# Two-layer MoE behind sliding-window attention on one core: twelve later attention pairs grouped two at a time in the same PSUM banks, values ahead of scores

## Chip, core and metric

The kernel runs on one core of a Trainium2 chip. Its time is the device time of one execution in microseconds (us); less is better. TensorE (PE) multiplies matrices into PSUM, which is split into banks; VectorE (DVE) and ScalarE (ACT) read PSUM and compute on SBUF; SyncE (SP) issues the DMAs.

## The reference

```
def _attn_ref(q, k, v):            # 4 batches, 8 heads, 576 positions, 64 per head
    scores = scale * q @ k^T       # heads 0 to 3: window of 32 positions; heads 4 to 7: 32 positions in steps of 4
    scores = where(mask, scores, -1e9); scores -= max(scores)
    attn = exp(scores); attn = attn / (sum(attn) + 1e-9)
    return attn @ v
def _moe_ref(x, w_in, w_out):      # 2304 tokens, 512 wide, 2048 hidden
    h = maximum(x @ w_in, 0)
    return h * h @ w_out
def _moe2_ref(x, w_in, w_out):
    h = x @ w_in
    return (h * cos(h)) @ w_out
```

The output is `_moe2_ref(_moe_ref(attention))`, all in float32.

## The kernel before, in words

**The products.** The tokens are cut into five blocks of 512, 384, 512, 512 and 384. For each layer and block the hidden dimension is walked in 16 slices `fc`. `product1` (L402) makes one slice of h from 12 matmuls, `middle` applies the activation on ACT and DVE, `product2` (L458) adds the slice into four banks of y with 12 matmuls; it is called in two halves of 6. A float32 product is three matmuls, because each operand is split into a high part (`xh`, `gh`, `w..hi`) and a remainder (`xl`, `gl`, `..lo`). The weights are split on the way in by `split_w`: a DVE chain (L153, L156, L159), a cast on ACT (L162) and a subtraction on DVE (L164). The first layer's 32 weight tiles are split while early attention and the first block run.

**Attention.** A unit is 192 positions of one pair of heads; a pair of units (`two_units(u)`, units u and u + 3) is worked on together. The six pairs of the first batch come ahead of the first block. The other 18, called later pairs here, are laid between the products of blocks one to four. Each runs in steps: scores (24 matmuls, L242, into two banks); mask and scale on DVE into the tile `p` (two instructions, L324), then a maximum (L328); exponentials on ACT (L333); normalisation (L340, L341, and L345 on ACT or L348 on DVE); three transposes (L355, one bank); a copy of them on ACT into a tile of its own, `pts` (L363); values (24 matmuls, L255, two banks); `tokens_out`, which casts the result into `xh` on ACT (L291) and writes the remainder `xl` on DVE (L294). A group of these matmuls between two big ones is called a burst below. The trace shows two records for each of the 24 matmuls, so a burst of 24 reads x48 there.

**Banks and tiles.** `bank()` hands out the four banks of pool `ps_h`, which scores, transposes, values and `product1` share. `p` and `pts` have one buffer each.

**Order.** Every step is an event with a time in units of slices: slice `fc` of block k starts at 16 k + fc. `PLACES` gives the start of each later pair; a pair's values stand 0.003 behind the scores of the pair after it, its transposes two slices after its own start (or half a slice ahead of the next pair), and the first half of `product2` at .5 of a slice, the second at .75. Between times 0 and 96 a scheduler may reorder instructions of an engine, except that the matmuls wrapped in `pe(...)` keep the program's order. Each engine then works through its list in order, and a semaphore wait holds what stands behind it.

Of the kernel before, what the change touches and what calls it, by code (L numbers as in the profile page):

```python
# [7 lines left out]
F32 = mybir.dt.float32  # L8
# [82 lines left out]
def attention_moe_moe(ctx: ExitStack, tc: tile.TileContext, units, windows, masks, w1, w2, out):  # L91
# [24 lines left out]
    def at(t, f, *a):  # L116
        events.append((t, len(events), f, a))
# [9 lines left out]
    def early(i):  # L127

        return dict(tag=f"w{NF - 1 - i // 2}_{1 - i % 2}", name="early")
# [53 lines left out]
    vals = {}  # L183
    early_units = [u for u in range(N_EARLY) if u // NG % 2 == 0]

    def load_unit(u):
        hp = u % UNITS // NG
        if u >= N_EARLY:
            t = upool.tile([P, UQ + UK], F32, tag="uq", name="uq")
# [22 lines left out]
    def bank():  # L212
        return ps_h.tile([P, 512], F32, tag="h", name="h")
# [16 lines left out]
    def mask_of(u):  # L230
        m0 = MASK_OF[u % UNITS // NG >= NPAIR // 2][u % NG] * HK
        return mask[:, m0:m0 + TPU * HK]
# [26 lines left out]
                            start=True, stop=True,  # L259
                        ))  # L260

    def pieces(u):

        b, hp, g = u // UNITS, u % UNITS // NG, u % NG
        p0 = g * TPU * QT
        done = 0
        while done < TPU * QT:
            if hp >= NPAIR // 2:
                r, i0 = divmod(p0 + done, S // DIL)
                n, step = min(TPU * QT - done, S // DIL - i0), DIL  # L270
                t0 = b * S + DIL * i0 + r
            else:
                n, step = TPU * QT - done, 1
                t0 = b * S + p0 + done
            k = max(i for i in range(NB) if STARTS[i] <= t0)
            t0 -= STARTS[k]
            n = min(n, -(-(SIZES[k] - t0) // step))
            yield k, slice(t0, t0 + (n - 1) * step + 1, step), slice(done, done + n)
            done += n

    def tokens_out(u, outs):

        c = u % UNITS // NG
        parts = []
        for n, pv in outs:
            for k, to, of in pieces(u):
                xh, xl = (t[:, c:c + n, to] for t in block(0, k))
                parts.append((xh, xl, pv[:, :, of]))
            c += n
# [6 lines left out]
    def two_units(u):  # L296

        us = u, u + NG
        first = u < N_EARLY
        at_y = early_units.index(u) if first else None  # L300
        T2 = 2 * TPU
        xs2 = [loaded.pop(i) for i in us]
        if u == 0:
            fill(7)
        banks = [bank() for _ in us]
        ss = [s[:, :TPU * HK] for s in banks]
        scores(ss, xs2, first)
        if first:
            for s in ss:
                nc.tensor.matmul(s, ident16, mask_of(u), start=False, stop=True)  # L310
            fill(FILL[0][at_y])
        yield
        nm = stat.tile([P, TPU, 2], F32, tag="nm", name="nm")
        if first:
            p = wpool.tile([P, TPU, 2, HK], F32, **early(PLACE["p", at_y % 3]))
            s = [tiles(s) for s in ss]
            for n in range(2):
                nc.vector.tensor_reduce(
                    out=nm[:, :, n], in_=s[n], axis=AX.X, op=ALU.max, negate=True)
            nc.vector.tensor_scalar(out=nm, in0=nm, scalar1=SCALE, scalar2=None, op0=ALU.mult)  # L320
        else:
            p = ppool.tile([P, TPU, 2, HK], F32, tag="p", name="p")
            for n, s in enumerate(ss):
                nc.vector.scalar_tensor_tensor(  # L324
                    out=p[:, :, n], in0=tiles(s), scalar=SCALE,
                    in1=tiles(mask_of(u)), op0=ALU.mult, op1=ALU.add)
            s = p[:, :, 0], p[:, :, 1]
            nc.vector.tensor_reduce(out=nm, in_=p, axis=AX.X, op=ALU.max, negate=True)  # L328
        yield
        sm = stat.tile([P, TPU, 2], F32, tag="sm", name="sm")  # L330
        for n in range(2):
            for i in range(TPU):
                nc.scalar.activation(  # L333
                    out=p[:, i, n], in_=s[n][:, i], func=AF.Exp,
                    scale=SCALE if first else 1.0, bias=nm[:, i, n:n + 1],
                    accum_out=sm[:, i, n:n + 1])
        yield
        rs = stat.tile([P, T2], F32, tag="rs", name="rs")
        flat = lambda t: t.rearrange("p i n -> p (i n)")
        nc.vector.tensor_scalar(out=rs, in0=flat(sm), scalar1=EPS, scalar2=None, op0=ALU.add)  # L340
        nc.vector.reciprocal(out=rs, in_=rs)  # L341
        p = p.rearrange("p i n k -> p (i n) k")
        if u in with_weights:
            for i in range(T2):
                nc.scalar.activation(  # L345
                    out=p[:, i, :], in_=p[:, i, :], func=AF.Copy, scale=rs[:, i:i + 1])
        else:
            nc.vector.tensor_tensor(  # L348
                out=p, in0=p, in1=rs.unsqueeze(2).to_broadcast([P, T2, HK]), op=ALU.mult)
        yield  # L350
        pt_bank = y_bank(0) if first else bank()
        pt = pt_bank[:, :UP]
        p = p.rearrange("p (i n) k -> p i (n k)", n=2)
        for i in range(TPU):
            pe(nc.tensor.transpose(pt[:, i * P:(i + 1) * P], p[:, i], ident))  # L355
        if first:
            fill(FILL[1])
        yield
        if first:
            pts = wpool.tile([P, UP], F32, **early(PLACE["pts", at_y % 2]))  # L360
        else:
            pts = ptpool.tile([P, UP], F32, tag="pts", name="pts")
        nc.scalar.copy(out=pts, in_=pt)  # L363
        yield
        if first:
            pv = ps_e.tile([P, 2, 512], F32, tag="e", name="e")[:, :, :UQ]
            pvs = [pv[:, n] for n in range(2)]
        else:
            pvs = [bank()[:, :UQ] for _ in us]
        values(pvs, vals.pop(u), pts.rearrange("p (i q) -> p i q", i=TPU))  # L370
        yield
        for _ in tokens_out(u, [(2, pv)] if first else [(1, pv.unsqueeze(1)) for pv in pvs]):
            if first:
                yield
        yield

    running = {}
# [145 lines left out]
    def needed(u):  # L523
        b, hp, g = u // UNITS, u % UNITS // NG, u % NG
        t = b * S + (g * TPU * QT if hp < NPAIR // 2 else 0)
        return max(i for i in range(NB) if STARTS[i] <= t)


    later = sorted(
        (u for u in range(N_EARLY, UNITS * B) if u % UNITS // NG % 2 == 0),  # L530
        key=lambda u: (needed(u), u))


    place = [t - 0.01 for t in PLACES]
    with_weights = {u for u, t in zip(later, place) if t < NF}

    def later_by(t, d):

# [9 lines left out]
        return t  # L548
    for u, times in zip(early_units, EARLY_TIMES):
        in_steps([before(t) for t in times], u, two_units, u)  # L550
    for i, u in enumerate(later):
        t, t2 = place[i:i + 2]
        tr = min(t + TRANS, t2 - 0.5)
        in_steps([t, *(later_by(t, d) for d in (0.15, 0.75, 0.8)), tr, later_by(tr, 0.1),
                  t2 + 0.003, later_by(t2, 0.42)], u, two_units, u)
        for n in range(2):
            at(later_by(t, -1.5 + 0.1 * n) if i else before(49), load_unit, u + n * NG)
        at(later_by(t, 0.6) if i else before(49), load_values, u)


    def some(table, i, times):
# [131 lines left out]
```

## Time and profile before

| what | value |
|---|---|
| median of 3 runs | 864.4 us (864.31 to 864.66) |
| profiled execution | 865.89 us; its span 864.1 us |
| PE busy | 852.7 us, 99% of the span |
| DVE busy | 505.5 us, 58% |
| ACT busy | 434.7 us, 50% |
| granted TensorE clock, mean | 0.996 of full speed |

The span runs from the first to the last instruction; the other 1.8 us lie around it. A busy PE here means that matmuls follow each other without a gap in the records; it does not say that each is useful. The 18 later pairs lie between 45 and 327 us of the span; behind that stand only products.

### The profile page before, as it was taken

What the parts mean: (1) busy time and instruction counts of PE and PEld (TensorE: products, weight loads), DVE (VectorE), ACT (ScalarE), POOL (GpSimd) and SP (SyncE); (2) the same over time, 40 slices, a digit from 0 to 9 for tenths busy, and PEclk for the clock granted to TensorE, in tenths of its full rate; (3) what the DMA queues carried; (4) which work ended last, traced back from release to release, by engine and by line L of the source; (5) the groups of instructions that cost most, each with busy time, mean ns of one, the idle gap of its engine ahead of it and who ended that gap; (6) DMA issues with size and microseconds to landing.
All of it is one profiled execution on the core that took longest, in us unless ns stands there. A gap on an engine that the chain in (4) does not pass through costs nothing.

```text
span 864.1 us, 15506 instructions
## 1 busy us (share of the span) xinstructions
PE 852.7 (99%) x6242; PEld 743.7 (86%) x6248; DVE 505.5 (58%) x980; ACT 434.7 (50%) x1061; POOL 47.9 (6%) x84
## 2 busy tenths in 40 slices
PE   7999999999999999999999999999999999999998
PEld 4778889999888888889999888899988888888998
DVE  5899954454443353225999974556555555555554
ACT  6667764443433332224555654555554545455554
POOL 0000000000000000000000110111111111111110
PEclk9899999999999999999999999999999999999999
DMA  7767612221311120003564400020020002000101
GB/s 285 260 218 268 229 59 90 75 78 39 102 52 39 36 98 1 1 1 132 193 229 153 152 19 1 22 77 1 1 86 1 0 1 86 1 0 1 50 1 37
DMA packets 24711, 68.59 MB, mean 79 GB/s; under 512 B 2624, under 2 KB 8512, under 8 KB 24640
## 3 DMA queue, kind: packets, MB, share of 16 engines
q1 hardware_dynamic: 24352, 67.38, 23.3%
q8 instruction: 49, 0.80, 0.4%
q10 hardware_dynamic: 288, 0.23, 0.1%
q14 instruction: 22, 0.18, 0.1%
HBM read 58.16 MB, written 9.44 MB: 78 GB/s over the span
## 4 chain that ended last, share of the span: by engine, by line
PE 95%; DVE 2%; ACT 1%; DMA 1%; issue 0%; SPq 0%
PE y L458 45%; PE h L402 44%; PE h L255 2%; PE h L242 2%; DMA early<-units 1%; PE h L355 1%; PE e L255 1%; DVE wt L159 1%; DVE wt L156 0%; DVE w L164 0%; ACT early L333 0%; PE y L355 0%; DVE wt L153 0%; DVE xl L294 0%; DVE gl L444 0%
## 5 line engine op out<-in xcount | busy, mean ns | idle before, releaser
L458 PE MATMUL y<-gh,w 128*128 128x512 f32 (+1 forms) x1280 | 401.6, 371 | 0.0
L402 PE MATMUL h<-xh,w 128*128 128x512 f32 (+1 forms) x1280 | 394.2, 369 | 0.0
L402 PEld LDWEIGHTS h<-xh,w 128*128 128x128 f32 x1280 | 238.2, 188 | 31.1 <-DVE p L324 0.4
L458 PEld LDWEIGHTS y<-gh,w 128*128 128x128 f32 x1280 | 237.6, 188 | 30.3
L402 PE MATMUL h<-xl,w 128*128 128x512 f32 (+1 forms) x640 | 235.8, 368 | 0.3 <-DVE xl L294 0.3
L458 PE MATMUL y<-gl,w 128*128 128x512 f32 (+1 forms) x640 | 235.3, 368 | 0.0
L444 DVE TENSOR_TENSOR gl<-r,gh 128x512 fp32r<-128x512 f32 (+1 forms) x160 | 102.5, 641 | 132.8 <-ACT gh L442 132.7
L433 DVE TENSOR_TENSOR r<-h,r 128x512 f32<-128x512 f32 (+1 forms) x128 | 81.9, 641 | 165.1 <-ACT r L430 94.6
L402 PEld LDWEIGHTS h<-xl,w 128*128 128x128 f32 x640 | 120.4, 188 | 16.0 <-DVE xl L294 0.7
L458 PEld LDWEIGHTS y<-gl,w 128*128 128x128 f32 x640 | 120.2, 188 | 14.3 <-DVE gl L444 0.2
L442 ACT CAST gh<-r 128x512 fp32r<-128x512 f32 (+1 forms) x160 | 92.3, 577 | 75.1 <-PE y L458 64.4
L429 ACT ACTIVATE r<-r 128x512 f32<-128x512 f32 (+1 forms) x80 | 47.1, 590 | 145.4 <-DVE r L426 145.4
L414 ACT ACTIVATE r<-h 128x512 f32<-128x512 f32 (+1 forms) x80 | 44.3, 554 | 96.8 <-PE h L402 96.6
L421 POOL TENSOR_SCALAR kf<-kf 128x512 f32<-128x512 f32 (+1 forms) x80 | 47.7, 596 | 805.3 <-ACT kf L420 801.8
L420 ACT ACTIVATE kf<-h,magic 128x512 f32<-128x512 f32 (+1 forms) x80 | 51.1, 639 | 21.8 <-PE h L402 21.6
L430 ACT ACTIVATE r<-r,halfpi 128x512 f32<-128x512 f32 (+1 forms) x80 | 54.3, 681 | 2.4
L424 DVE SCALAR_TENSOR_TENSOR r<-kf,h 128x512 f32<-128x512 f32 (+1 forms) x80 | 49.9, 625 | 4.7 <-POOL kf L421 4.7
L426 DVE SCALAR_TENSOR_TENSOR r<-kf,r 128x512 f32<-128x512 f32 (+1 forms) x80 | 50.9, 638 | 2.5
L162 ACT CAST w<-wt 128x512 fp32r<-128x512 f32 x64 | 39.4, 619 | 24.5 <-DVE wt L159 24.4
L164 DVE TENSOR_TENSOR w<-wt,w 128x512 fp32r<-128x512 f32 x64 | 43.4, 684 | 5.2 <-ACT w L162 5.1
L159 DVE SCALAR_TENSOR_TENSOR wt<-wraw,wt 128x512 uint32<-128x512 uint32 x58 | 40.4, 699 | 0.3
L156 DVE SCALAR_TENSOR_TENSOR wt<-wraw,wt 128x512 uint32<-128x512 uint32 x58 | 39.9, 689 | 0.8
(55 smaller groups left out, 395.3 us busy)
## 6 DMA issues: line engine op xcount, KB each, us to landing
wraw<-w SPq DMA_DIRECT2D x58, 512.0 KB, 4.0
uq<-units SPq DMA_DIRECT2D x36, 208.0 KB, 3.6
uv<-windows SPq DMA_DIRECT2D x18, 384.0 KB, 4.6
early<-w SPq DMA_DIRECT2D x6, 512.0 KB, 4.4
y<-o SPq DMA_DIRECT2D x6, 512.0 KB, 2.8
xraw<-y SPq DMA_DIRECT2D x6, 512.0 KB, 5.0
out<-o SPq DMA_DIRECT2D x6, 512.0 KB, 2.8
early<-units SPq DMA_DIRECT2D x6, 416.0 KB, 6.1
```

The source lines that it names most:

```text
L159: nc.vector.scalar_tensor_tensor(out=t, in0=low, scalar=29, in1=t, op0=ALU.logical_shift_right, op1=ALU.bitwise_or)
L402: pe(nc.tensor.matmul(h, w[:, c * P:(c + 1) * P], x[:, c, :], start=c == 0 and i == 0, stop=c == NC - 1 and i == 2))
L420: nc.scalar.activation(out=kf, in_=h, func=AF.Identity, bias=magic, scale=INV2PI)
L421: nc.gpsimd.tensor_scalar(out=kf, in0=kf, scalar1=-MAGIC, scalar2=1.0, op0=ALU.add, op1=ALU.mult)
L424: nc.vector.scalar_tensor_tensor(out=r, in0=kf, scalar=-C1, in1=h, op0=ALU.mult, op1=ALU.add)
L426: nc.vector.scalar_tensor_tensor(out=r, in0=kf, scalar=-C2, in1=r, op0=ALU.mult, op1=ALU.add)
L429: nc.scalar.activation(out=r, in_=r, func=AF.Abs)
L430: nc.scalar.activation(out=r, in_=r, func=AF.Sin, bias=halfpi, scale=-1.0)
L433: nc.vector.tensor_tensor(out=r, in0=h, in1=r, op=ALU.mult)
L442: nc.scalar.copy(out=gh, in_=r)
L444: nc.vector.tensor_tensor(out=gl, in0=r, in1=f32(gh), op=ALU.subtract)
L458: pe(nc.tensor.matmul(y[e], w[:, e * P:(e + 1) * P], g, start=fc == 0 and n == 0, stop=fc == NF - 1 and n == 2,))
```

## The change

Twelve of the later pairs form six groups of two; six stay single: 12, 13, 18, 19, 20 and 38. A function `group(us)` takes the place of `two_units` for later pairs. A group's two units share two banks for scores and two for values; their transposes take a bank each. The tile `pts` is gone: transposes are copied back into `p`, which holds one or two pairs and still has one buffer. Values are called 0.003 ahead of the next group's scores. `PLACES` has 13 entries in place of 19, and the first six are the old ones. The transposes' time is now the start plus one slice and one for each pair. For a single pair whose successor starts two slices later, that time lies just behind the values' time; as the steps of a pair are resumed in order, the step resumed ahead of the next scores is then the transposes, and values follow 0.1 of a slice later. Normalisation of the fifth and sixth later pairs goes to DVE. Every later pair's exponentials, copies and stores remain, in other batches.

```diff
-PLACES = (3.75, 6.75, 8.75, 10.75, 12.75, 14.75, 17.75, 20.75, 22.75, 25.75, 27.75, 30.75, 33.75, 36.75, 39.75, 42.75, 45.75, 48.75, 51.75)
-TRANS = 2
+GROUPS = ((12,), (13,), (18,), (19,), (20,), (14, 24), (30, 31), (32, 25), (26, 36), (42, 43), (44, 37), (38,))
+PLACES = (3.75, 6.75, 8.75, 10.75, 12.75, 14.75, 20.75, 25.75, 30.75, 36.75, 42.75, 46.75, 51.75)
...
-    ptpool = pool("pt", 1)
...
+    def group(us):
+
+        parts = [slice(a * TPU, (a + 1) * TPU) for a in range(len(us))]
+        ss = [bank()[:, :len(us) * TPU * HK] for _ in range(2)]
+        for u, i in zip(us, parts):
+            scores([s[:, i.start * HK:i.stop * HK] for s in ss],
+                   [loaded.pop(n) for n in (u, u + NG)], False)
+        yield
+        p = ppool.tile([P, len(us) * TPU, 2, HK], F32, tag="p", name="p")
+        nm = stat.tile([P, len(us) * TPU, 2], F32, tag="nm", name="nm")
+        for n, s in enumerate(ss):
+            for u, i in zip(us, parts):
+                nc.vector.scalar_tensor_tensor(
+                    out=p[:, i, n], in0=tiles(s)[:, i], scalar=SCALE,
+                    in1=tiles(mask_of(u)), op0=ALU.mult, op1=ALU.add)
+        nc.vector.tensor_reduce(out=nm, in_=p, axis=AX.X, op=ALU.max, negate=True)
+        yield
+        sm = stat.tile([P, len(us) * TPU, 2], F32, tag="sm", name="sm")
+        for i in parts:
+            exponentials(p[:, i], (p[:, i, 0], p[:, i, 1]), nm[:, i], sm[:, i], 1.0)
+            yield
+            normalize(rows_of(p[:, i]), flat(sm[:, i]), us in with_weights)
+            yield
+        pts = [bank()[:, :UP] for _ in us]
+        for pt, i in zip(pts, parts):
+            transposes(pt, p[:, i])
+        yield
+        for pt, i in zip(pts, parts):
+            nc.scalar.copy(out=p[:, i].rearrange("p i n k -> p (i n k)"), in_=pt)
+        yield
+        pvs = [bank()[:, :len(us) * UQ] for _ in range(2)]
+        for a, (u, i) in enumerate(zip(us, parts)):
+            values([pv[:, a * UQ:(a + 1) * UQ] for pv in pvs], vals.pop(u),
+                   p[:, i].rearrange("p i n k -> p i (n k)"))
+        yield
+        for _ in tokens_out(us, [(1, pv.unsqueeze(1)) for pv in pvs]):
+            pass
         yield
...
-    with_weights = {u for u, t in zip(later, place) if t < NF}
+    with_weights = {us for us, t in zip(GROUPS, place) if t < NF - 4}
...
-    for i, u in enumerate(later):
+    for i, us in enumerate(GROUPS):
         t, t2 = place[i:i + 2]
-        tr = min(t + TRANS, t2 - 0.5)
-        in_steps([t, *(later_by(t, d) for d in (0.15, 0.75, 0.8)), tr, later_by(tr, 0.1),
-                  t2 + 0.003, later_by(t2, 0.42)], u, two_units, u)
...
+        by = lambda d: later_by(t, d)
+        soft = [by(0.15)] + [by(d + a) for a in range(len(us)) for d in (0.75, 0.8)]
+        tr = t + 1 + len(us)
+        in_steps([t, *soft, tr, later_by(tr, 0.1), t2 - 0.003, later_by(t2, 0.42)],
+                 us, group, us)
```

In the order of the engines' lists the change reads as follows; names are those of the kernel. PE first, where the third later pair's scores come in (in the kernel before, at 78 us of the trace): the rows before.

```order
L458 MATMUL y_795<-gh,w_1_1025 128x512
L458 MATMUL y_795<-gl,w_1_1025 128x512
L458 MATMUL y_795<-gh,w_1_1025 128x512
L242 MATMUL h<-uq 32x64 x24
L255 MATMUL h<-pts,uv 64x32 x24
L458 MATMUL y_796<-gh,w_1_1025 128x512
L458 MATMUL y_796<-gl,w_1_1025 128x512
L458 MATMUL y_796<-gh,w_1_1025 128x512
L458 MATMUL y_797<-gh,w_1_1025 128x512
L458 MATMUL y_797<-gl,w_1_1025 128x512
L458 MATMUL y_797<-gh,w_1_1025 128x512
L402 MATMUL h<-xh_364,w_0_1048 128x512
```

And the same place after the change: the second half of `product2` (L497 in the changed file) ends a slice, and `product1` (L441) begins the next.

```order
L335 MATMUL h<-ident,p 128x128 x3
L241 MATMUL h<-uq 32x64 x24
L497 MATMUL y_793<-gh,w_1_1021 128x512
L497 MATMUL y_793<-gl,w_1_1021 128x512
L497 MATMUL y_793<-gh,w_1_1021 128x512
L497 MATMUL y_794<-gh,w_1_1021 128x512
L497 MATMUL y_794<-gl,w_1_1021 128x512
L497 MATMUL y_794<-gh,w_1_1021 128x512
L254 MATMUL h<-p,uv 64x32 x24
L441 MATMUL h<-xh_361,w_0_1044 128x512
L441 MATMUL h<-xl_362,w_0_1044 128x512
```

The transposes moved from ahead of the first half of that `product2` to the burst, and the values from the burst to the end of the slice, directly ahead of `product1`. This holds at four places: behind the scores of the third, fourth and fifth later pair and of the first group of two. With the waits shown, the end of that piece reads so (`DVE_49` is the semaphore that DVE raises, `Activation_49` that of ACT):

```order
L497 MATMUL y_794<-gh,w_1_1021 128x512
L254 MATMUL h<-p,uv 64x32 [waits DMAHW3_49,Activation_49]
L254 MATMUL h<-p,uv 64x32
L254 MATMUL h<-p,uv 64x32 [waits PE_49]
L254 MATMUL h<-p,uv 64x32 x21
L441 MATMUL h<-xh_361,w_0_1044 128x512 [waits DVE_49]
L441 MATMUL h<-xl_362,w_0_1044 128x512
```

In the kernel before, `product1` at this place also waits for DVE, but half a `product2` stands between it and the burst. The instruction that raises DVE's semaphore here is the first of the two that read the new scores' banks into `p`. On DVE, before the change, they stand so (L324, with waits; the L156, L159 and L153 rows around them split weights):

```order
L156 SCALAR_TENSOR_TENSOR wt<-wraw,wt 128x512 [waits DVE_49]
L153 TENSOR_SCALAR wt<-wraw 128x512 [waits DMAHW6_49,DVE_49]
L159 SCALAR_TENSOR_TENSOR wt<-wraw,wt 128x512 [waits DVE_49]
L324 SCALAR_TENSOR_TENSOR p<-h,given 128x3x64 [waits PE_49] x2
L156 SCALAR_TENSOR_TENSOR wt<-wraw,wt 128x512 [waits DVE_49]
L328 TENSOR_REDUCE nm<-p 128x6 [waits DVE_49]
```

After the change (L389 are the same two instructions; L152, L155, L158 and L163 split weights):

```order
L155 SCALAR_TENSOR_TENSOR wt<-wraw,wt 128x512 [waits DVE_49]
L152 TENSOR_SCALAR wt<-wraw 128x512 [waits DMAHW6_49,DVE_49]
L158 SCALAR_TENSOR_TENSOR wt<-wraw,wt 128x512 [waits DVE_49]
L155 SCALAR_TENSOR_TENSOR wt<-wraw,wt 128x512 [waits DVE_49]
L158 SCALAR_TENSOR_TENSOR wt<-wraw,wt 128x512 [waits DVE_49]
L163 TENSOR_TENSOR w_0_1227<-wt,w_0_1227 128x512 [waits Activation_49]
L389 SCALAR_TENSOR_TENSOR p<-h,given 128x3x64 [waits PE_49]
L389 SCALAR_TENSOR_TENSOR p<-h,given 128x3x64
L483 TENSOR_TENSOR gl<-r,gh 128x512 [waits Activation_49]
```

Three more weight-splitting instructions stand ahead of the two, and the two wait for the last of PE's values, as they write `p`, from which the values are read. At the next such place, the fourth later pair's, the remainder `gl` of the slice (L483) stands directly ahead of them, and it waits for ACT's cast `gh`:

```order
L155 SCALAR_TENSOR_TENSOR wt<-wraw,wt 128x512 [waits DVE_49]
L163 TENSOR_TENSOR w_1_1510<-wt,w_1_1510 128x512 [waits Activation_49]
L483 TENSOR_TENSOR gl<-r,gh 128x512 [waits Activation_49]
L389 SCALAR_TENSOR_TENSOR p<-h,given 128x3x64 [waits PE_49]
L389 SCALAR_TENSOR_TENSOR p<-h,given 128x3x64
```

At the fifth pair's place the row ahead of the two is the same `gl`; at that of the first group of two it is the same `gl` once more, and there are four such instructions instead of two, two for each bank.

Counted over PE's list, the bursts of the later pairs change as follows. Before there are 37: 18 of transposes alone, 17 of scores and values, one of scores alone and one of values alone. After there are 25: one of scores (the first pair), two of transposes (the first pair's and the last pair's), six of a group's transposes, four of transposes and scores, four of values alone (the four places above), one of a single pair's values with the next scores, five of a group's values with the next group's scores, one of a group's values with the last pair's scores, and one of values (the last pair's). In blocks two to four nothing but these bursts differs on PE.

## Rows read from the trace of the kernel before

**Rows 1.** The page, busy time of each engine (share of the span) and instructions.

```profile
PE 852.7 (99%) x6242; PEld 743.7 (86%) x6248; DVE 505.5 (58%) x980; ACT 434.7 (50%) x1061; POOL 47.9 (6%) x84
```

**Rows 2.** Windows: length, busy PE, PEld, DVE, ACT, POOL, granted clock, DMA share, GB/s.

```profile
65.00:87.00 22.00, 22.00 (x276) 17.87 (x260) 21.93 (x51) 16.83 (x55) 0.00 (x0) 1.00 0.78 263
...
109.00:131.00 22.00, 22.00 (x193) 18.43 (x192) 10.79 (x26) 14.50 (x53) 0.00 (x0) 1.00 0.14 43
```

**Rows 3.** Timeline of PE: start, length, operation; from one big matmul to another.

```profile
70.56 0.39 PE L402 MATMUL h<-xh,w 128*128 128x512 f32 x1
...
73.28 0.39 PE L458 MATMUL y<-gh,w 128*128 128x512 f32 x1
73.51 0.39 PE L402 MATMUL h<-xh,w 128*128 128x512 f32 x1
...
148.76 0.33 PE L458 MATMUL y<-gl,w 128*128 128x384 f32 x1
148.93 0.34 PE L458 MATMUL y<-gh,w 128*128 128x384 f32 x1
```

**Rows 4.** Timeline of PE: scores alone, between two big matmuls and behind.

```profile
45.43 0.39 PE L458 MATMUL y<-gh,w 128*128 128x512 f32 x1
45.75 0.75 PE L242 MATMUL h<-uq 64*32 64x64 f32 x48
46.44 0.50 PE L458 MATMUL y<-gh,w 128*128 128x512 f32 x1
46.77 0.40 PE L458 MATMUL y<-gl,w 128*128 128x512 f32 x1
```

**Rows 5.** Timeline of PE: scores and values in one burst, and what follows.

```profile
64.78 0.76 PE L242 MATMUL h<-uq 64*32 64x64 f32 x48
65.46 0.90 PE L255 MATMUL h<-pts,uv 64*64 64x32 f32 x48
66.30 0.50 PE L458 MATMUL y<-gh,w 128*128 128x512 f32 x1
...
67.56 0.40 PE L458 MATMUL y<-gh,w 128*128 128x512 f32 x1
67.93 0.50 PE L402 MATMUL h<-xh,w 128*128 128x512 f32 x1
```

**Rows 6.** Timeline of PE: transposes alone, ahead of the third later scores.

```profile
76.00 0.39 PE L402 MATMUL h<-xh,w 128*128 128x512 f32 x1
76.23 0.49 PE L355 MATMUL h<-ident,p 128*128 128x128 f32 x3
76.47 0.48 PE L458 MATMUL y<-gh,w 128*128 128x512 f32 x1
76.79 0.39 PE L458 MATMUL y<-gl,w 128*128 128x512 f32 x1
```

**Rows 7.** Timeline of DVE: masking instructions (L324); releaser in brackets.

```profile
67.53 0.35 DVE L324 SCALAR_TENSOR_TENSOR p<-h,given 128x192 f32<-128x192 f32 x1
...
79.42 0.68 DVE L159 SCALAR_TENSOR_TENSOR wt<-wraw,wt 128x512 uint32<-128x512 uint32 x1
80.02 0.61 DVE L324 SCALAR_TENSOR_TENSOR p<-h,given 128x192 f32<-128x192 f32 x2
80.55 0.68 DVE L156 SCALAR_TENSOR_TENSOR wt<-wraw,wt 128x512 uint32<-128x512 uint32 x1
...
117.78 0.62 DVE L324 SCALAR_TENSOR_TENSOR p<-h,given 128x192 f32<-128x192 f32 x2 [1.81 <-PE h L242]
```

**Rows 8.** Timeline of PE: the scores that the last masking row waits for.

```profile
117.02 0.76 PE L242 MATMUL h<-uq 64*32 64x64 f32 x48
```

**Rows 9.** Timeline of ACT and DVE: the chain from `gh` to `gl`.

```profile
73.76 0.62 ACT L442 CAST gh<-r 128x512 fp32r<-128x512 f32 x1 [0.42 <-PE y L458]
...
108.30 0.61 ACT L442 CAST gh<-r 128x512 fp32r<-128x512 f32 x1
...
108.94 0.69 DVE L444 TENSOR_TENSOR gl<-r,gh 128x512 fp32r<-128x512 f32 x1 [0.18 <-ACT gh L442]
109.55 0.69 DVE L156 SCALAR_TENSOR_TENSOR wt<-wraw,wt 128x512 uint32<-128x512 uint32 x1
```

**Rows 10.** Timeline of ACT and DVE: storing one pair's values.

```profile
92.66 0.86 ACT L291 CAST xh<-h 128x80 fp32r<-128x80 f32 x6 [0.93 <-PE h L255]
...
94.72 1.00 DVE L294 TENSOR_TENSOR xl<-h,xh 128x80 fp32r<-128x80 f32 x5
```

More of the change, by code (lines that the diff above doesn't have):

```diff
@@ L294, in tokens_out, with normalize, exponentials @@
             nc.vector.tensor_tensor(out=xl, in0=piece, in1=f32(xh), op=ALU.subtract)
[L296 to L320, printed above, removed]
-        else:
[L322 to L330, printed above, removed]
+    def normalize(p, sm, by_scalar):
+        n = p.shape[1]
+        rs = stat.tile([P, n], F32, tag="rs", name="rs")
+        nc.vector.tensor_scalar(out=rs, in0=sm, scalar1=EPS, scalar2=None, op0=ALU.add)
+        nc.vector.reciprocal(out=rs, in_=rs)
+        if by_scalar:
+            for i in range(n):
+                nc.scalar.activation(
+                    out=p[:, i, :], in_=p[:, i, :], func=AF.Copy, scale=rs[:, i:i + 1])
+        else:
+            nc.vector.tensor_tensor(
+                out=p, in0=p, in1=rs.unsqueeze(2).to_broadcast([P, n, HK]), op=ALU.mult)
+    def exponentials(p, s, nm, sm, scale):
         for n in range(2):
@@ L334, in two_units @@
                     out=p[:, i, n], in_=s[n][:, i], func=AF.Exp,
[L335 to L353, printed above, removed]
+                    scale=scale, bias=nm[:, i, n:n + 1], accum_out=sm[:, i, n:n + 1])
@@ L354, in two_units, with transposes @@
+    flat = lambda t: t.rearrange("p i n -> p (i n)")
+    rows_of = lambda p: p.rearrange("p i n k -> p (i n) k")
+    def transposes(pt, p):
+        p = p.rearrange("p i n k -> p i (n k)")
         for i in range(TPU):
             pe(nc.tensor.transpose(pt[:, i * P:(i + 1) * P], p[:, i], ident))
-        if first:
-            fill(FILL[1])
-        yield
[L359 to L362, printed above, removed]
+    def two_units(u):
+        us = u, u + NG
+        at_y = early_units.index(u)
+        xs2 = [loaded.pop(i) for i in us]
+        if u == 0:
+            fill(7)
+        ss = [bank()[:, :TPU * HK] for _ in us]
+        scores(ss, xs2, True)
+        for s in ss:
+            nc.tensor.matmul(s, ident16, mask_of(u), start=False, stop=True)
+        fill(FILL[0][at_y])
+        yield
+        nm = stat.tile([P, TPU, 2], F32, tag="nm", name="nm")
+        p = wpool.tile([P, TPU, 2, HK], F32, **early(PLACE["p", at_y % 3]))
+        s = [tiles(s) for s in ss]
+        for n in range(2):
+            nc.vector.tensor_reduce(
+                out=nm[:, :, n], in_=s[n], axis=AX.X, op=ALU.max, negate=True)
+        nc.vector.tensor_scalar(out=nm, in0=nm, scalar1=SCALE, scalar2=None, op0=ALU.mult)
+        yield
+        sm = stat.tile([P, TPU, 2], F32, tag="sm", name="sm")
+        exponentials(p, s, nm, sm, SCALE)
+        yield
+        normalize(rows_of(p), flat(sm), False)
+        yield
+        pt = y_bank(0)[:, :UP]
+        transposes(pt, p)
+        fill(FILL[1])
+        yield
+        pts = wpool.tile([P, UP], F32, **early(PLACE["pts", at_y % 2]))
@@ L363, in two_units @@
         nc.scalar.copy(out=pts, in_=pt)
         yield
[L365 to L370, printed above, removed]
-        yield
-        for _ in tokens_out(u, [(2, pv)] if first else [(1, pv.unsqueeze(1)) for pv in pvs]):
-            if first:
-                yield
+        pv = ps_e.tile([P, 2, 512], F32, tag="e", name="e")[:, :, :UQ]
@@ L550, in attention_moe_moe @@
         in_steps([before(t) for t in times], u, two_units, u)
-    for i, u in enumerate(later):
+    for i, us in enumerate(GROUPS):
         t, t2 = place[i:i + 2]
-        tr = min(t + TRANS, t2 - 0.5)
-        in_steps([t, *(later_by(t, d) for d in (0.15, 0.75, 0.8)), tr, later_by(tr, 0.1),
-                  t2 + 0.003, later_by(t2, 0.42)], u, two_units, u)
-        for n in range(2):
-            at(later_by(t, -1.5 + 0.1 * n) if i else before(49), load_unit, u + n * NG)
-        at(later_by(t, 0.6) if i else before(49), load_values, u)
+        by = lambda d: later_by(t, d)
[3 more added lines that the diff above has]
+                 us, group, us)
+        for a, u in enumerate(us):
+            for n in range(2):
+                at(by(-1.5 + 0.1 * (2 * a + n)) if i else before(49), load_unit,
+                   u + n * NG, "uv" if a and n else "uq")
+            at(by(0.6 + 0.1 * a) if i else before(49), load_values, u)
     def some(table, i, times):
```

72 lines of the change are left out of this document (42 added, 30 removed).

## Prediction

> **What bounds the kernel now.** I read the page's busy times first: PE is busy 852.7 of 864.1 us, no other engine over 60% [rows 1]. So the change can gain only what it takes from PE's own list, and lose wherever PE is made to wait. I then read PE's timeline around attention. Big matmuls follow each other every 0.227 us in blocks of 512 (70.56 to 73.28 is 2.72 us for 12) and every 0.17 us in blocks of 384 [rows 3]. Between them a burst of scores starts 0.32 us after the big matmul before it, 0.09 more than that pace, takes 0.69 us, and the first big matmul behind it takes 0.33, 0.10 more [rows 4]. In a burst of both, values take 0.84 and follow the scores with no gap of their own [rows 5]. Transposes start at the big matmul's own pace, take 0.24 us, and cost 0.09 at the exit (0.32 for the next one) [rows 6]. So a burst costs a switch, and fewer bursts cost fewer switches. Last I read windows: between 65 and 87 us, where the third later pair stands, DVE is busy 21.93 of 22.00 us with weights; after 109 us it is half idle [rows 2]. A new wait of PE for DVE in the first stretch therefore has no slack behind it. The clock is 1.00 of full speed in both, so it moves nothing here.
>
> **The change, part by part.** *Removed switches.* Bursts of transposes alone fall from 18 to 8: ten exits of 0.09, 0.90 us. Bursts with scores or values fall from 19 to 17: two entries and exits of 0.09 + 0.10, 0.38 us. Together 1.28 us. The trace has no burst that passes from transposes to scores or from values to scores, so the price of that seam is bounded: free, as from scores to values, or an entry of 0.09 each. Eleven seams hold here (four of the first kind, seven of the second); at 0.09 each 0.99 less, so the gain lies between 0.3 and 1.3 us. I take 1.28, since the seam that the trace does show is free. The matmuls themselves stay: as many of each kind as before, and double bursts run longer at the same price. Copies and stores come in other batches on ACT and DVE, which are not the bound.
>
> *Added waits.* At four places the order is now transposes, scores, six matmuls of `product2`, values, `product1`. `product1` takes a bank of the new scores, which the first masking instruction on DVE must have read; and that instruction writes `p`, from which the values ahead of it are being read. Before, transposed values had a tile of their own, so masking ran while `product2` did. Now PE cannot begin `product1` until the values are done and masking has then run: values, masking, `product1` in series. All of PE stands behind that `product1`.
>
> The floor of that wait: masking starts when the last of the values ends, and the end of a modelled burst lies 0.07 us behind the start of the next big matmul (scores at 117.02 + 0.76 = 117.78, where masking starts [rows 7, 8]; the same burst in rows 4 gives 0.69 to the next matmul). From the start of masking to the start of `product1` it is 0.40 us: 67.53 to 67.93, where PE waited for just that at the second pair (0.37 us from the matmul before in place of 0.23) [rows 5, 7]. So no less than 0.47 us each. For the group of two there are two masking instructions on that first bank, and the first takes 0.27 (two in 0.53, 80.02 to 80.55 [rows 7]), so 0.74. Floor of all four: 3 x 0.47 + 0.74 = 2.15 us.
>
> What stands ahead of masking on DVE makes it longer. *Third pair:* before, masking began at 80.02, directly behind a weight instruction that began at 79.42, 0.60 earlier; DVE was full. Three more such instructions now stand ahead: 80.02 + 3 x 0.60 = 81.82, and `product1` at 82.22. Without the wait it would stand at 76.23 + 1.36 (six matmuls) + 0.24 + 0.09 + 0.69 + 0.10 + 1.36 + 0.09 + 0.84 = 81.00. Wait: 1.22 us. *Fourth and fifth pair:* `gl` stands ahead of masking and waits for the cast `gh`, which waits for the end of the six `product2` matmuls. Call the start of what follows these six h. The cast began 0.25 behind it (73.51 to 73.76) and runs 0.61; `gl` follows 0.03 later (108.30 + 0.61 to 108.94) and the next DVE instruction 0.61 after that (109.55) [rows 3, 9]. Masking at h + 0.25 + 0.62 + 0.03 + 0.61 = h + 1.51, `product1` at h + 1.91, where values alone would let it start at h + 0.09 + 0.84 = h + 0.93. Wait: 0.98 us each. *First group:* the same with 0.27 more, 1.25 us. Sum: 1.22 + 0.98 + 0.98 + 1.25 = 4.43 us. If DVE has one weight instruction more ahead at each place, that is 4 x 0.60 = 2.4 us more; the floor is 2.15. While PE waits, DVE and ACT work on, so the wait is not paid twice: `gl` and the activation of the next slice come no later to PE than PE itself does.
>
> A repeated gap of this sort has a line in the notes: the Trainium skill, Perfetto Trace Analysis, Identifying Performance Opportunities, says that the same gap repeating on the engine that should be saturated can mean too little SBUF or PSUM for the next tile. The trace before has no such gap on PE around the later pairs, and by that rule the one buffer of `p` would make one.
>
> *Later blocks.* Behind the first group values stand directly ahead of scores, and masking of the new scores has half a `product2` to run beside, as before. I cost those bursts at nothing; what that rests on is the third rival.
>
> **Sum.** 4.43 - 1.28 = 3.15 us on the profiled execution: 865.89 + 3.15 = 869.0. The median of the runs shown, 864.4, lies 1.5 below that execution, so 867.6 as the median after. I call 0.2% (1.73 us, 862.7 to 866.1) what a measurement here can tell from no change.
>
> **Rivals.** *Four waits of about 1 us each:* the forecast, 867.6. For it speaks that the wait is in the program, whatever the timing, and that its links are rows.
>
> *Short waits, the other side.* Place: masking behind values at the same four places. If DVE has cleared its list by then, so that only the series values, masking, `product1` is left, the waits are 2.15 us and the switches give back 1.28: +0.87, 865.3, no measurable change. Below 3.0 us of waits in all (0.75 each) the time lies within 0.2%; below 1.28 us (0.32 each) the kernel would be no slower at all, and that is under the floor. For it speaks that DVE has less to do behind 109 us; against it that `gl` there hangs on PE's own matmuls through ACT, not on DVE's load, and that at the third pair DVE has 0.07 us free in 22. Faster by over 0.2% would need no waits and more than 1.73 us from the switches, which the sum does not give; that would take some wait of before that I have not seen.
>
> *Late banks in the later blocks.* A group's values for two pairs lie in two banks, and `product1` half a slice later takes the first of them. It must have been read by casts (six in 0.86 us) and subtractions (five in 1.00, so six in 1.2) [rows 10]: about 2.1 us. PE covers that with scores of two pairs, 2 x 0.69, an exit of 0.10 and six matmuls of 0.17, 2.5 us, less 0.07 for the end of the values. That leaves 0.35 us. If one other instruction of 0.6 us stands ahead on ACT or DVE, PE waits 0.25; if two do, 0.85; over five such bursts 1.3 to 4.3 us, which makes 868.9 to 871.9. Against it: only blocks of 384 are so tight; six matmuls of 0.227 leave 0.34 more, and DVE is half idle there. A page speaks for this rival: the Trainium skill, Perfetto Trace Analysis, Matmuls (under Optimizing Tensor Performance), wants independent groups of matmuls to rotate through banks, so that reading one overlaps the next group's matmuls. Two pairs in one bank rotate less, and no row here shows what that costs.
>
> **How the numbers follow.** Four waits of about 1 us: 0.62, at 866.3 to 869.3. Short waits: 0.22, 864.9 to 866.1. Late banks on top of the four waits: 0.10. Something that makes it faster: 0.06. The range reaches from the floor's case, less 0.4 us for a larger gain at the switches, 864.9, to the forecast with one more instruction of 0.6 us at each place, 867.6 + 2.4 = 870.0, which takes in the smaller part of the late banks. Slower by over 0.2% is the first and third case, 0.72; within 0.2% the second, 0.22; faster the last, 0.06.
>
> **What would show it.** In the profile after, PE's timeline has four gaps ahead of `product1` between 78 and 135 us, each released by DVE's masking instruction, about 1.2, 1.0, 1.0 and 1.2 us, with values directly ahead of the gap and masking beginning at or after the end of the values. Transposes directly ahead of scores and values directly ahead of scores show no more than 0.1 us between them; 25 bursts cost some 1.3 us less than 37. No PE idle with a releaser stands behind 140 us; if there is, on a bank that ACT's casts or DVE's subtractions let go, it is the third rival. The prediction is wrong if masking begins within 0.1 us of the values' end at all four places (short waits), or if PE's gaps there are missing altogether, which would mean that the bank came from somewhere else than I read.

## The result and the profile after

The changed kernel takes 872.5 us (871.16 to 873.35, 6 runs) beside 864.6 us of the kernel before (6 runs): ratio 1.0086, interval 1.0074 to 1.0098. It is slower, as forecast, but by 7.9 us, more than twice the 3.2 that was forecast. The profiled execution, at 872.67 us, has a span of 870.9 us, 6.8 more than before. Busy times, by engine:

```profile
PE 851.6 (98%) x6242; PEld 743.5 (85%) x6248; DVE 503.4 (58%) x970; ACT 432.7 (50%) x1043; POOL 48.0 (6%) x84
```

PE is busy 1.1 us less than in [rows 1] and has as many instructions. So the loss is idle time of PE. The list of who PE waited for (engine, line, releaser: total us, times, longest) begins so:

```profile
PE h L441 <- DVE p L389: 5.0, 5, 1.3
PE h L241 <- issue: 2.9, 2, 1.7
PE e L254 <- issue: 1.6, 2, 1.5
```

The first line is `product1` waiting for masking. The second is new and was not forecast: scores that stop for 2.9 us in two places, released by nothing that the profile shows. (The third lies in the first 25 us, ahead of all that the change touches, where PE waits in several ways that differ from one execution to the next; its longest, 1.47 us at 22.19, comes up again below.)

**The masking gaps** stand where they were forecast. PE at the first of the four places, in order of time:

```profile
78.21 0.39 PE L497 MATMUL y<-gh,w 128*128 128x512 f32 x1
78.44 0.49 PE L335 MATMUL h<-ident,p 128*128 128x128 f32 x3
78.86 0.76 PE L241 MATMUL h<-uq 64*32 64x64 f32 x48
79.55 0.50 PE L497 MATMUL y<-gh,w 128*128 128x512 f32 x1
...
81.13 0.90 PE L254 MATMUL h<-p,uv 64*64 64x32 f32 x48
83.19 0.50 PE L441 MATMUL h<-xh,w 128*128 128x512 f32 x1 [1.16 <-DVE p L389]
```

Values take 0.84 us, so `product1` would have begun at 81.97 and is 1.22 late. DVE at the first, second and fourth place:

```profile
82.18 0.68 DVE L163 TENSOR_TENSOR w<-wt,w 128x512 fp32r<-128x512 f32 x1
82.78 0.61 DVE L389 SCALAR_TENSOR_TENSOR p<-h,given 128x192 f32<-128x192 f32 x2
...
96.62 0.69 DVE L483 TENSOR_TENSOR gl<-r,gh 128x512 fp32r<-128x512 f32 x1
97.22 0.62 DVE L389 SCALAR_TENSOR_TENSOR p<-h,given 128x192 f32<-128x192 f32 x2
...
125.64 0.69 DVE L483 TENSOR_TENSOR gl<-r,gh 128x512 fp32r<-128x512 f32 x1 [6.50 <-ACT gh L481]
126.25 1.14 DVE L389 SCALAR_TENSOR_TENSOR p<-h,given 128x192 f32<-128x192 f32 x4
```

Masking runs directly behind a weight instruction or behind `gl`, and `product1` starts 0.41 us after masking (82.78 to 83.19; 0.40 in [rows 5, 7]). At the fourth place DVE had been idle 6.5 us for `gh`.

**The new stalls** lie in bursts of two groups, 96 records of values and 96 of scores. The first such burst and the second:

```profile
154.23 0.34 PE L497 MATMUL y<-gh,w 128*128 128x384 f32 x1
154.50 1.60 PE L254 MATMUL h<-p,uv 64*64 64x32 f32 x96
156.03 1.03 PE L241 MATMUL h<-uq 64*32 64x64 f32 x75
158.24 0.43 PE L241 MATMUL h<-uq 64*32 64x64 f32 x21 [1.17 <-issue]
158.60 0.44 PE L497 MATMUL y<-gh,w 128*128 128x384 f32 x1
...
180.03 0.34 PE L497 MATMUL y<-gh,w 128*128 128x384 f32 x1
180.30 1.60 PE L254 MATMUL h<-p,uv 64*64 64x32 f32 x96
181.83 1.27 PE L241 MATMUL h<-uq 64*32 64x64 f32 x96
183.03 0.44 PE L497 MATMUL y<-gh,w 128*128 128x384 f32 x1
```

The first takes 4.37 us from one big matmul to the next, the second 3.00: 1.37 lost, after 75 of 96 records of scores. The third, at 204.78, stops after 74 for 1.68 us and loses 1.88 (4.88 in all); the fourth and fifth don't stop. No wait on a semaphore stands at these places in PE's list: the 38th of 48 matmuls is like those around it.

What is under way there is PE's own program. The page's part on DMA queues (packets, MB, share) has a row for instructions:

```profile
q8 instruction: 49, 0.80, 0.4%
```

The DMA view of 155.8 to 156.9 us, within that burst, has one of these transfers:

```profile
q8 instruction: 1, 0.02, 5.3%
```

It is one packet, on one of the 16 engines, so it took 5.3% of 16 x 1.1 us, 0.93 us; by the trace's packets it began at 155.88 and landed at 156.81. The page has 49 transfers of 16 KB. PE has 12,490 records of matmuls and weight loads, 255 for each transfer. The Trainium skill, Runtime: NRT & Kernel Launch, Instruction fetch mechanics, says that instructions come in blocks of 16 KiB, 256 each, the next fetched while the current one runs, mostly hidden. By these rows the size agrees, and hidden is what has to be tested. Counted in program order (a small float32 matmul of attention is four instructions, two weight loads and two matmuls; a big one two; a wait of its own one), the two stalls begin at PE's instructions 3,778 and 5,058: 1,280 apart, 5 x 256. (The trace has 3,772 and 5,052 records of PE ahead of them; six matmuls have left no record.) So block ends are known for every burst. A burst of two groups has 386 instructions; the first block end in it is its 87th, 215th, 85th, 163rd and 244th in the five bursts. Only in the first and third does a second one fall into the same burst, 256 later, and only these stall.

The kernel before had a small sign of it, in early attention. PE there, and at the same place after the change:

```profile
21.91 0.24 PE L255 MATMUL e<-early 64*64 64x32 f32 x2 [0.17 <-issue]
```

```profile
22.19 0.24 PE L254 MATMUL e<-early 64*64 64x32 f32 x2 [1.47 <-issue]
```

955 records of PE stand ahead of either, which is within one of 3,772 less 11 x 256, so a block end fits there too.

### The profile page after: what moved, and what is told of

Same layout as the page of the kernel before. It is cut to its first block, busy times and chain, and to the rows that moved or that the text cites. A ratio compares the mean times of both kernels' runs of the same rounds, so it can differ in the third digit from the quotient of the medians.

```text
span 870.9 us, 15484 instructions
## 1 busy us (share of the span) xinstructions
PE 851.6 (98%) x6242; PEld 743.5 (85%) x6248; DVE 503.4 (58%) x970; ACT 432.7 (50%) x1043; POOL 48.0 (6%) x84
## 4 chain that ended last, share of the span: by engine, by line
PE 88%; DVE 7%; DMA 2%; issue 2%; ACT 1%; SPq 0%; ACTq 0%; DVEq 0%
PE y L497 42%; PE h L441 42%; DVE wt L158 2%; DVE wt L155 2%; DVE w L163 1%; PE h L254 1%; PE h L241 1%; DMA early<-units 1%; DVE wt L152 1%; DVE gl L483 1%; DMA early<-windows 1%; PE h L335 1%; DMA wraw<-w 0%; PE e L254 0%; DVE xl L306 0%
## 5 line engine op out<-in xcount | busy, mean ns | idle before, releaser
L441 PE MATMUL h<-xh,w 128*128 128x512 f32 (+1 forms) x1280 | 394.6, 369 | 5.0 <-DVE p L389 5.0
L497 PE MATMUL y<-gh,w 128*128 128x512 f32 (+1 forms) x1280 | 397.9, 369 | 0.0
L441 PEld LDWEIGHTS h<-xh,w 128*128 128x128 f32 x1280 | 238.1, 188 | 36.5 <-DVE p L389 4.5
L497 PEld LDWEIGHTS y<-gh,w 128*128 128x128 f32 x1280 | 237.5, 188 | 30.5
L441 PE MATMUL h<-xl,w 128*128 128x512 f32 (+1 forms) x640 | 235.8, 368 | 0.3 <-DVE xl L306 0.3
L497 PE MATMUL y<-gl,w 128*128 128x512 f32 (+1 forms) x640 | 235.4, 368 | 0.0
L483 DVE TENSOR_TENSOR gl<-r,gh 128x512 fp32r<-128x512 f32 (+1 forms) x160 | 102.5, 641 | 128.0 <-ACT gh L481 126.6
L441 PEld LDWEIGHTS h<-xl,w 128*128 128x128 f32 x640 | 120.4, 188 | 15.8 <-DVE xl L306 0.7
L497 PEld LDWEIGHTS y<-gl,w 128*128 128x128 f32 x640 | 120.2, 188 | 15.1 <-DVE gl L483 0.6
L163 DVE TENSOR_TENSOR w<-wt,w 128x512 fp32r<-128x512 f32 x64 | 43.3, 685 | 4.8 <-ACT w L161 4.5
L325 ACT ACTIVATE p<-p,nm 128x64 f32<-128x64 f32 x108 | 36.2, 337 | 9.5 <-DVE nm L392 9.5
L158 DVE SCALAR_TENSOR_TENSOR wt<-wraw,wt 128x512 uint32<-128x512 uint32 x58 | 40.4, 700 | 0.4
```

What stands on the lines that cost most here:

```text
L158: nc.vector.scalar_tensor_tensor(out=t, in0=low, scalar=29, in1=t, op0=ALU.logical_shift_right, op1=ALU.bitwise_or)
L163: nc.vector.tensor_tensor(out=lo, in0=f32(t), in1=f32(hi), op=ALU.subtract)
L441: pe(nc.tensor.matmul(h, w[:, c * P:(c + 1) * P], x[:, c, :], start=c == 0 and i == 0, stop=c == NC - 1 and i == 2))
L483: nc.vector.tensor_tensor(out=gl, in0=r, in1=f32(gh), op=ALU.subtract)
L497: pe(nc.tensor.matmul(y[e], w[:, e * P:(e + 1) * P], g, start=fc == 0 and n == 0, stop=fc == NF - 1 and n == 2,))
```

## Experiments

Theory A, after the traces: the one buffer `p` puts values, masking and `product1` in series (gaps), and bursts of 386 small instructions outrun the fetch of PE's program (stalls). Rivals: B, DVE is full, whatever `p` does; C, the stalls come from the loads of units and windows that start in these bursts; D, values ahead of scores make masking late by themselves. Seven kernels, each timed beside the kernel before; ratios are to that one's runs on the same chip (its medians there are 866.1 and 866.3 us).

**Transposes in a tile of their own again**, for single pairs:

```diff
+    ptpool = pool("pt", 1)
...
+        q = ptpool.tile([P, TPU, 2, HK], F32, tag="pts", name="pts") if len(us) == 1 else p
         for pt, i in zip(pts, parts):
-            nc.scalar.copy(out=p[:, i].rearrange("p i n k -> p (i n k)"), in_=pt)
+            nc.scalar.copy(out=q[:, i].rearrange("p i n k -> p (i n k)"), in_=pt)
...
-                   p[:, i].rearrange("p i n k -> p i (n k)"))
+                   q[:, i].rearrange("p i n k -> p i (n k)"))
```

> The changed kernel, but the transposes of a single pair are copied into a tile of their own again, as in the kernel before; groups of two still copy into p. Theory A (one buffer p, read by the values, holds masking back, and product1 behind it): masking then stands right behind the scores in DVE's list and no longer waits for the values, so the four gaps of 1.16, 1.18, 1.08 and 1.28 us ahead of product1 fall to under 0.2 us each, and the time falls by 4 to 4.7 us, to about 868. The two stalls without a releaser at 158 and 209 us stay, some 4.5 us earlier. Rival B (the gaps come from a full DVE and from where values stand, not from p): the gaps stay at 0.7 us or more, and the time falls by less than 2 us.

867.1 us, ratio 1.0004 (0.9993 to 1.0015): no loss is left that can be told from noise. PE's waits for masking are gone entirely, and two stalls of 1.74 and 1.24 us remain at 152.97 and 203.34. PE and DVE at the first and second place:

```profile
80.24 0.90 PE L255 MATMUL h<-pts,uv 64*64 64x32 f32 x48
81.08 0.50 PE L443 MATMUL h<-xh,w 128*128 128x512 f32 x1
```

```profile
79.96 0.61 DVE L390 SCALAR_TENSOR_TENSOR p<-h,given 128x192 f32<-128x192 f32 x2
...
92.49 0.60 DVE L390 SCALAR_TENSOR_TENSOR p<-h,given 128x192 f32<-128x192 f32 x2
...
94.68 0.68 DVE L485 TENSOR_TENSOR gl<-r,gh 128x512 fp32r<-128x512 f32 x1
```

Values still stand directly ahead of `product1`, and no gap follows. DVE is as full as before (busy 21.93 us of 22.00 from 65 to 87, as in [rows 2]), but masking now runs ahead of the values, and the scheduler put it ahead of `gl` too. B falls.

**Transposes half a slice ahead of the next pair**, so that values and scores share a burst:

```diff
-        tr = t + 1 + len(us)
+        tr = min(t + 1 + len(us), t2 - 0.5)
```

> The changed kernel, but a single pair's transposes stand no later than half a slice ahead of the next pair, as before, so that its values share the burst of the next scores, values first, with half a product2 behind them; p is still copied into in place. Theory A: the four gaps of 1.1 to 1.3 us ahead of product1 fall to what the second pair shows in the changed kernel, 0.3 us each, since scores now end a burst and masking has 1.36 us of matmuls beside it; the switches of four bursts fewer give 0.1 to 0.2 us each, less four exits of transposes of 0.09. Sum: 4.7 - 1.3 = 3.4 us, and some 0.3 us: about 869. The stalls without a releaser in the first and third burst of two groups stay. Rival B (masking is late whatever stands around it because DVE is full): the gaps stay above 0.8 us, 871 or more.

867.0 us, ratio 1.0006 (0.9995 to 1.0017). The gaps fell to nothing, not to 0.3 us; the stalls were 1.23 and 1.13 us. Here `p` is still written in place: with half a `product2` behind the scores, masking has its time. The two kernels take the same loss away from either end of the series.

**Values ahead of scores in the kernel before**, nothing else:

```diff
-                  t2 + 0.003, later_by(t2, 0.42)], u, two_units, u)
+                  t2 - 0.003, later_by(t2, 0.42)], u, two_units, u)
```

> The kernel before with one edit: values stand ahead of the next scores in all of its bursts; pairs stay single and the tile of their own for transposes stays. Theory A (the order inside a burst costs nothing where half a product2 follows it): the time is within 0.2% of the kernel before, and product1 behind the bursts beside the first block starts without a gap of over 0.2 us. Rival D (scores that end later make masking late for product1, as the 0.32 us at the second pair of the changed kernel suggests): 0.3 us at each of the five bursts beside the first block, 1.5 us more.

867.2 us, ratio 1.0010 (0.9998 to 1.0021). The time alone leaves room for D's 1.5 us, but PE has no gap of over 0.2 us behind any of these bursts: D falls. The 0.32 us at the second pair of the changed kernel doesn't belong to the order: with the same instructions up to there, the kernel of the next experiment shows no gap that the list of waits names.

**Values of a group half a `product2` ahead of the next scores:**

```diff
-        in_steps([t, *soft, tr, later_by(tr, 0.1), t2 - 0.003, later_by(t2, 0.42)],
+        in_steps([t, *soft, tr, later_by(tr, 0.1), t2 - (0.25 if len(us) > 1 else 0.003), later_by(t2, 0.42)],
```

> The changed kernel, but a group's values stand half a product2 (6 matmuls) ahead of the next scores, not in their burst. Theory A (PE's instructions come in blocks of 256, fetched by DMA; a burst of 386 that crosses two block boundaries uses up a block in 1.9 us while the next takes 3.0 to 3.6 us to come): 6 matmuls between the halves give 1.04 us (384) to 1.36 us (512) and an entry and exit of 0.19, so the stalls of 1.17 and 1.68 us without a releaser shrink to 0 to 0.5 us; six more switches cost 6 x 0.19 = 1.1 us. Sum: 3.25 - 1.1 - 0.3 = 1.9 us less, 870.6 (870.0 to 871.4). Rival C (the loads of units and windows that start in those bursts hold PE up): the stalls stay at over 1 us, as the loads start at the same places, and the time rises by 1.1 us to 873.6.

870.5 us, ratio 1.0049 (1.0031 to 1.0067), span 868.6, 2.3 us under the changed kernel's. No scores wait for "issue" any more; the masking gaps stay:

```profile
PE h L441 <- DVE p L389: 4.7, 4, 1.3
PE h L241 <- DMA early<-units: 2.5, 3, 1.7
```

(The second line lies in the first 25 us.) The first burst's scores take 1.48 us in place of 1.27, so about 0.2 of its stall is left. Rival C would have kept the stalls.

**Block ends moved by 104 instructions**, put at the very start of PE's list:

```diff
-            fill(7)
+            fill(2)
+            for _ in range(57):
+                nc.tensor.matmul(spare[:, :16], idle[:, :P], idle[:, :16], start=True, stop=True)
```

> The changed kernel with 104 more small instructions on PE at the very start (5 of the 7 warm-up matmuls of 512 columns are replaced by 57 of 16 columns); nothing else moves. Theory A (block boundaries at every 256th instruction): a group's burst of 386 instructions stalls if its first boundary lies within its first 130. In the changed kernel the first boundary lies at 87, 215, 85, 163 and 244 in the five bursts of two groups, and the first and third stall. With 104 more it lies at 239, 111, 237, 59 and 140: the second and fourth stall, by 1.2 to 1.8 us (near 181 and 242 us), and the first and third no longer do. The time stays within 1 us of the changed kernel's. Rival C (loads, or what those two bursts wait for in data): the first and third burst still stall, and the second and fourth don't.

873.3 us, ratio 1.0086 (1.0062 to 1.0110). The stalls moved as forecast, from the first and third burst to the second and fourth:

```profile
180.79 0.34 PE L241 MATMUL h<-uq 64*32 64x64 f32 x9 [1.31 <-issue]
240.41 0.60 PE L241 MATMUL h<-uq 64*32 64x64 f32 x35 [1.71 <-issue]
280.54 0.39 PE L499 MATMUL y<-gh,w 128*128 128x512 f32 x1 [0.30 <-issue]
```

The second block end lies at 111 + 256 = 367 of 386 in the second burst, which leaves 19 instructions or 9.5 records (9 were left), and at 59 + 256 = 315 in the fourth, which leaves 71, 35.5 records (35). In the fifth it lies at 140 + 256 = 396, ten behind the burst, and there a big matmul waits 0.30 us. The trace has 4,540 and 5,820 records of PE ahead of the first two of these stalls; like 3,772 and 5,052, each is 188 more than a multiple of 256. The loads start in all five bursts of both kernels, whether they stall or not. C falls as the cause of the stalls. The fetch was not hidden at these places.

**Masking ahead of `gl`**, by a later time for `gl` in slices 7 to 14 of the first block and by pinning both in DVE's list:

```diff
-                steady = ([0] * (NC - 1), MIDDLE[m], (LAG[m] + 0.5, LAG[m] + 0.75))
+                mid = MIDDLE[m] if (m, k) != (0, 0) or fc not in range(7, 15) else (0.53, 0.72, 0.86, 1.93)
+                steady = ([0] * (NC - 1), mid, (LAG[m] + 0.5, LAG[m] + 0.75))
```

> The changed kernel, but DVE's list is held so that masking at the four places stands ahead of the remainder gl (two weight instructions still stand there); p is still read by the values and written by masking. Theory A (values, masking, product1 in series is the floor, and gl ahead of masking is the rest): the gaps at the second to fourth place fall from 1.18, 1.08 and 1.28 us to the floor, 0.5 to 0.8 us each, but not to 0; the first, where weight instructions stand ahead, falls by 0.3 us at most. Sum 1.3 to 1.9 us less than the changed kernel. If gl alone were the cause, the gaps at these three would go to under 0.2 us; if p alone, they would stay at 1.0 or more.

870.9 us, ratio 1.0060 (1.0041 to 1.0078). The gaps were 1.36, 0.56, 1.02 and 0.93 us, 3.9 in all in place of 4.7 at the four places; 1.3 to 1.9 less was expected. (The profiled execution took 874.5, with two stretches at a lower clock that the last section shows.) The fourth shows the series bare: DVE idle for 8.38 us, then masking on the heels of the values, and still

```profile
126.26 1.15 DVE L390 SCALAR_TENSOR_TENSOR p<-h,given 128x192 f32<-128x192 f32 x4 [8.38 <-PE h L254]
```

```profile
125.19 0.90 PE L254 MATMUL h<-p,uv 64*64 64x32 f32 x48
127.02 0.47 PE L442 MATMUL h<-xh,w 128*128 128x512 f32 x1 [0.93 <-DVE p L390]
```

a gap of 0.93 (0.99 from start of values plus 0.84), where the forecast put the floor at 0.74. At the third, weight instructions took the room of `gl`. So the floor exists; what stood on it was whatever DVE had next, and reordering DVE alone took only 0.8 us of these gaps. (By the ratios this kernel lies some 2.2 us below the changed one, with intervals that touch; the gaps account for 0.8 of it.)

**The better kernel**: transposes early as above, and values half a `product2` ahead of the scores only in the two bursts with two block ends:

```diff
-        tr = t + 1 + len(us)
-        in_steps([t, *soft, tr, later_by(tr, 0.1), t2 - 0.003, later_by(t2, 0.42)],
+        tr = min(t + 1 + len(us), t2 - 0.5)
+        in_steps([t, *soft, tr, later_by(tr, 0.1), t2 - (0.25 if i in (5, 7) else 0.003), later_by(t2, 0.42)],
```

> The changed kernel with two edits: a single pair's transposes stand half a slice ahead of the next pair, as before (this took away the four gaps behind masking), and values stand half a product2 ahead of the next scores, but only in the two bursts that cross two block boundaries of PE's instructions (those with the first and the third group of two). Theory A: no gap behind masking and no stall without a releaser; against that kernel without the split, 1.23 + 1.13 = 2.4 us of stalls go and two switches of 0.19 come: 2.0 us less, 865.0 beside 866.1 of the kernel before, so 1 to 2 us below it. Rival C (the stalls belong to what those bursts load or wait for): stalls of over 0.5 us remain, and the time stays at 867.

864.2 us beside 866.3 of the kernel before, ratio 0.9979 (0.9970 to 0.9987): faster than both kernels. One stall of 0.53 us is left in the first of the two split bursts; in the other the scores take 1.58 us in place of 1.27, so 0.3 is left there.

## Why the prediction was right and wrong

*Right:* slower, and by the mechanism named. `product1` came 1.22, 1.24, 1.14 and 1.34 us late at the four places (start of values plus 0.84, against its start), 4.9 in all, where the sum had 1.22, 0.98, 0.98, 1.25, 4.43. At the second and third place `gl` waited for DVE, not for ACT: the cast at the second began at 95.72 and was done at 96.34, `gl` began at 96.62, when DVE's weight instructions let it. So it is partly luck that 0.98 came near 1.24 and 1.14 there. The late banks of the third rival did not come: the list has no wait of PE behind the first block that names ACT's casts or DVE's subtractions. Nor did the short waits.

*Mis-sized:* the switches. I had 1.28 us; taking every burst as the time from the last big matmul ahead of it to the second one behind it, beyond their pace, and the gaps and stalls out, bursts of the later pairs cost 37.2 us before and 34.9 after, 2.3 less. The seam from transposes to scores is not free: 78.44 to 78.86 is 0.42, where transposes alone take 0.24, so it costs exit and entry in full. Six transposes in two banks cost as much as two times three. The seam from values to scores is free (65.28 to 66.11 at the second pair, 0.83). And "double bursts run longer at the same price" was wrong to the good: 96 records of values take 1.53 us, not 1.68, and 96 of scores 1.20 (181.83 to 183.03), not 1.38. I did not find why.

*The step that failed* is "I cost those bursts at nothing" for the later blocks, whose only rival was late banks. The sign named for those blocks was idle time with a releaser; what came has none. In its place, bursts of 386 instructions outrun the fetch of PE's program: the first block end is crossed near 155.2 us (87 of the 192 instructions of values, at 1.53 us for all), the transfer shows between 155.8 and 156.9, PE has used up the next block at 157.06 and starts again at 158.24, some 3.0 us after the crossing. It uses a block in 1.9 us in such a burst. In the kernel before no burst of the later pairs has more than 194 instructions, so no two block ends fall into one. That gave 1.37 + 1.88 = 3.25 us. Two kernels show it: the stalls move with the count of instructions, and all but go when six big matmuls stand between.

*The sum on the profiled executions:* 4.9 - 2.3 + 3.25 = 5.9 us; the second pair's gap and the first 58 us of this execution add 0.35 and 0.49, and 0.1 is unassigned, to 6.8. The 0.35 and the 0.49 are no part of the change as far as the runs show: the gap is in no other kernel's list, and the first later pair's transposes begin at 58.09 us before and at 58.58 after, and at 57.39 to 59.10 in six other kernels whose lists are the same up to there. The medians are 7.9 apart, 1.1 more, as the profiled execution before, 865.89 us, lies 1.3 above the median of its six runs, and the one after 0.15 above its own.

*From crossing to restart:* the transfer begins 0.7 us after the crossing in the first burst, takes 0.93, and PE restarts 1.4 after it has landed (156.81 to 158.24). In the third burst the restart came 3.6 us after the crossing, and the difference is the transfer: it began at 206.18, 0.8 after the crossing, and its row in the DMA view of 206.1 to 207.7 reads

```profile
q8 instruction: 1, 0.02, 5.6%
```

5.6% of 16 x 1.6 us is 1.43; it landed at 207.60, and PE restarted at 209.02, again 1.4 later. At all the stalls of scores of two groups, in the six kernels that have them, the restart lies 1.3 to 1.5 us behind the landing.

*Open:* what fills these 1.4 us, the profile doesn't show. Loads of windows ran beside the longer transfer; whether these made it longer wasn't tried apart, since the loads start when the burst frees their buffers.

## What to carry to other kernels

A tile that is reused in place gets a second reader, and the next write waits for it: follow what that write holds up, here a bank and through it all of PE; and look at which of the two ends is easier to move. Where many tiny matmuls are joined into longer bursts, count PE's instructions: a burst in which two ends of 256-instruction blocks fall stalled here for 1.1 to 1.7 us, and six big matmuls between its halves were cover enough for most of that.

## What the runs showed of the hardware that was not expected

PE's clock can fall behind a gap of this size. In the kernel with masking ahead of `gl`, after the gap of 1.36 us at the first place, and in the one with shifted block ends, after the stall of 1.71 us, big matmuls ran for some 3.4 us at 0.43 us each, where 0.227 is their pace. It came a second time in the first of these kernels, around the end of a stall of 1.59 us without a releaser. Windows of the three, in this order (columns as in [rows 2]):

```profile
84.00:86.00 2.00, 2.00 (x6) 1.54 (x6) 2.00 (x5) 1.66 (x10) 0.00 (x0) 0.50 0.76 248
```

```profile
242.00:244.00 2.00, 2.00 (x6) 1.52 (x6) 1.17 (x3) 0.71 (x2) 0.00 (x0) 0.50 0.99 341
```

```profile
159.00:161.90 2.90, 2.90 (x29) 2.73 (x11) 2.10 (x5) 0.32 (x1) 0.00 (x0) 0.50 0.96 345
```

The granted clock is 0.50, which is the lower of its levels, 1.2 of 2.4 GHz, with PE busy all the time. It fell 0.9 and 1.3 us after PE had started again in the first two, and 0.1 us before it in the third. Each cost about 1.7 us beside the gap itself, half of the 3.4; the two in the profiled execution with masking ahead of `gl` make 3.4, and that execution, at 874.5 us, lies 3.5 above its kernel's median. It did not follow every gap: the profiled execution of the changed kernel has gaps of 1.08 to 1.68 us from 83 us on and a clock of 1.00 behind each. Which gap it takes, these runs don't settle; it makes a gap on PE dearer than its length at times. That it also makes executions of a kernel with such gaps more uneven fits these numbers but was not tried apart.
